# Gathered rows of seven experts turned by DMA instead of TensorE

## The chip, the cores and the metric

The kernel runs on one core of a Trainium2 chip. The metric is the device time of one execution in microseconds; before the change the median of three runs is 1160.86 us (1159.09 to 1165.01).

## What is computed

Three layers follow each other: attention over 4 x 12 heads of 448 x 64, a dense layer with an ELU between its two matrices, and a layer of eight experts. Only the last one matters here:

```python
def _moe2_ref(x, w_gate, w1, w2):          # x (1792, 768), E = 8, F = 1024
    cap = N // E                            # 224 tokens for every expert
    ...                                     # greedy assignment by logits
    for e in range(E):
        mask = assigned == e
        h = np.maximum(x[mask] @ w1[e], 0.0)
        out[mask] = h @ w2[e]
```

## The kernel before

Every float32 factor is split into two float16 numbers, a high and a low one, and a product is made of three float16 products (high by high, low by high, high by low). The rows of x stand in DRAM as `x2_d[0]` and `x2_d[1]`, each with 384 of the 768 columns, high halves first and low halves behind them, so a row of one of them has 768 float16 numbers.

The loop over the experts (lines 974 to 979) does this for each expert `e`:

- `load_expert(e + 1)` brings w1 and w2 in 14 float32 pieces (six of 512 KB, eight of 384 KB) on SP's queue into three staging buffers `st`. ACT (line 350) writes each piece's high half, DVE (line 351) its low half; DVE's instruction frees the staging buffer. There are two sets of weight buffers for odd and even experts, so w1 of expert e + 1 can be written once the first products of expert e - 1 are over, and w2 once its second products are.
- `gather(e + 1)` fetches 224 rows in four parts, `i` (which of the two column halves) by `hh` (which 112 tokens). For each part POOL issues an indirect DMA into one of four buffers `xg` (112 tokens x 768), TensorE turns six blocks of 112 x 128 into the PSUM tile `pte`, and one copy (ACT where hh is 0, DVE where it is 1) brings them to `xT[i]`, named `xTe` in the profile. `xT[i]` has two buffers, so that of expert e + 1 is the one that expert e - 1 has used.
- `expert(e)` makes the first products `phe` (144 matmuls of 224 columns, in four steps of 36; each step needs one of two PSUM tiles, which `relu` on ACT, line 941, and DVE, line 942, reads into `hT`), then the second products `pye` (96 matmuls in two halves), which ACT and DVE copy to `yo` (lines 965 and 966) and POOL scatters to the output (line 967).

Expert 0 is special: its first products run in two halves, because its second column half arrives late.

Nobody writes the order on an engine by hand. A scheduler simulates the program and puts each engine's instructions in a fixed order; an instruction that comes earlier in the program goes first where several are ready. Each engine and each queue then runs its instructions strictly in that order, and waits at the first one that isn't ready. SP's queue carries all weight pieces of this stage. Transposing DMAs on that queue are in use already in the attention stage, at lines 490 (`kT`, `qT`) and 614 (`wt`, 128 rows of 768).

Of the kernel before, what the change touches and what calls it, by code (L numbers as in the profile page):

```python
# [255 lines left out]
def kernel(  # L256
# [14 lines left out]
    nc = tc.nc  # L271
# [19 lines left out]
    HD = CAP // 2  # L291
# [39 lines left out]
    def tr16(o, i, n):  # L331
        mm(o, i, id16[:n, :n], is_transpose=True, start=True, stop=True)
# [404 lines left out]
    for b in range(B):  # L737
        xT = big.tile([P, KC, 2, S], F16, name="xT")
        for hp in range(0, NP, 2):
            d = Duo(b, hp, xT)  # L740
            t = (b * NP + hp) * PR
# [150 lines left out]
    def load_expert(e):  # L892
        if e == 0:
            hold.append(R.marks[0])
        pool = wuB if e % 2 else wuA
        W1 = pool.tile([P, 2, KC, F1], F16, tag="wu", name=f"w1_{e}")
        W2 = pool.tile([P, 2, NF1, DM], F16, tag="wu", name=f"w2_{e}")
        for c in range(KC):
            load_split(W1[:, 0, c, :], W1[:, 1, c, :], w1[e, c * P:(c + 1) * P, :])
        for c in range(NF1):  # L900
            load_split(W2[:, 0, c, :], W2[:, 1, c, :], w2[e, c * P:(c + 1) * P, :])
        return W1, W2

    def gather(e):

        xT = [exg.tile([P, 2, KH, CAP], F16, name=f"xTe{i}") for i in range(2)]
        for i in range(2):
            for hh in range(2):
                xg = exg.tile([HD, 2, DH], F16, name="xg", bufs=4)
                POOL.indirect_dma_start(  # L910
                    out=xg.rearrange("p z d -> p (z d)"), out_offset=None, in_=x2_d[i],
                    in_offset=bass.IndirectOffsetOnAxis(ap=idx[:, 0, 2 * e + hh:2 * e + hh + 1], axis=0))
                pt = psX.tile([P, 2, KH, HD], F16, tag="pt", name="pte")
                for z in range(2):
                    for c in range(KH):
                        tr16(pt[:, z, c, :], xg[:, z, c * P:(c + 1) * P], HD)
                (DVE.tensor_copy if hh else ACT.copy)(xT[i][:, :, :, hh * HD:(hh + 1) * HD], pt)  # L917
        return xT
# [3 lines left out]
    def expert(e, W1, W2, xT):  # L922
# [33 lines left out]
        for hh in range(2):  # L956
# [15 lines left out]
            stores.append(st)  # L972

    W, xT = load_expert(0), gather(0)
    for e in range(NE):
        W_, x_ = W, xT
        if e + 1 < NE:
            W, xT = load_expert(e + 1), gather(e + 1)
        expert(e, *W_, x_)
# [30 lines left out]
```

## Time and profile before

| | us |
|---|---|
| median of three runs | 1160.86 |
| profiled execution, its own time | 1164.11 |
| its span, first to last instruction | 1162.4 |
| PE busy | 1039.3 |
| DVE busy | 784.2 |
| ACT busy | 539.2 |
| POOL busy | 353.9 |
| mean granted clock of TensorE | 0.963 of 2.4 GHz |

In the profile PE is TensorE's matmuls, PEld its weight loads, DVE VectorE, ACT ScalarE, POOL GpSimd and SP SyncE, which here only issues DMAs. A time in brackets behind an instruction is how long its engine stood idle before it, and what ended that. The experts run from about 895 us to the end of the span.

### The profile page before, as it was taken

What the parts mean: (1) busy time and instruction counts of PE and PEld (TensorE: products, weight loads), DVE (VectorE), ACT (ScalarE), POOL (GpSimd) and SP (SyncE); (2) the same over time, 40 slices, a digit from 0 to 9 for tenths busy, and PEclk for the clock granted to TensorE, in tenths of its full rate; (3) what the DMA queues carried; (4) which work ended last, traced back from release to release, by engine and by line L of the source; (5) the groups of instructions that cost most, each with busy time, mean ns of one, the idle gap of its engine ahead of it and who ended that gap; (6) DMA issues with size and microseconds to landing.
All of it is one profiled execution on the core that took longest, in us unless ns stands there. A gap on an engine that the chain in (4) does not pass through costs nothing.

```text
span 1162.4 us, 19353 instructions
## 1 busy us (share of the span) xinstructions
PE 1039.3 (89%) x7030; PEld 608.4 (52%) x7030; DVE 784.2 (67%) x1567; ACT 539.2 (46%) x1099; POOL 353.9 (30%) x462
## 2 busy tenths in 40 slices
PE   0687879897989999999999699999999898999997
PEld 0233334343444445444444345555546687888885
DVE  3788898999988775554337777877775565556520
ACT  2676677776777664554430410011102455555520
POOL 3687775757746451220000000000000412222100
PEclk9888889998999989999999899999999899999999
DMA  6355575569997825336823641030003778778710
GB/s 172 78 133 132 147 207 151 145 178 255 245 256 195 194 68 121 81 95 225 328 55 113 194 167 50 21 130 21 22 21 101 239 236 263 223 244 258 237 47 24
DMA packets 190319, 176.48 MB, mean 152 GB/s; under 512 B 114704, under 2 KB 161808, under 8 KB 189456
## 3 DMA queue, kind: packets, MB, share of 16 engines
q1 hardware_dynamic: 186064, 163.78, 49.5%
q0 software_dynamic: 3328, 11.01, 3.0%
q8 instruction: 55, 0.90, 0.3%
q10 hardware_dynamic: 832, 0.46, 0.1%
q14 instruction: 40, 0.33, 0.1%
HBM read 125.92 MB, written 31.98 MB: 136 GB/s over the span
## 4 chain that ended last, share of the span: by engine, by line
PE 48%; DVE 16%; DMA 13%; issue 10%; ACT 6%; POOL 4%; SPq 2%; POOLq 0%; DVEq 0%; ACTq 0%
PE py L324 17%; PE ph L324 12%; DMA st<-in_moe_w_dram 7%; PE po L324 4%; PE pye L324 3%; PE phe L324 3%; PE ps L324 3%; PE rt_pc L324 2%; DVE w L351 2%; DVE sm L533 2%; ACT w L350 2%; DVE cv L377 2%; PE pta L324 2%; DMA qn<-in_q_dram 2%; PE pl L324 1%
## 5 line engine op out<-in xcount | busy, mean ns | idle before, releaser
L324 PE MATMUL ph<-xT,w_in 128*128 128x448 f16 x1152 | 246.1, 358 | 8.2 <-DVE elu_g L685 5.2
L324 PE MATMUL py<-w_out,g 128*128 128x384 f16 x1152 | 204.5, 329 | 0.0
L324 PEld LDWEIGHTS <-w_in 128*128 128x128 f16 x1152 | 107.7, 99 | 127.7 <-issue 46.1
L351 DVE SCALAR_TENSOR_TENSOR w<-st,w 128x768 f16<-128x768 f32 (+1 forms) x112 | 119.2, 1072 | 76.7 <-ACT w L350 71.5
L545 POOL TENSOR_SCALAR pe<-pe,sm 128x448 f32<-128x448 f32 x168 | 126.7, 764 | 138.8 <-DVE sm L541 70.3
L324 PEld LDWEIGHTS <-g 128*128 128x128 f16 x1152 | 107.4, 98 | 89.3 <-issue 26.7
L324 PE MATMUL ps<-kT,qT 64*128 64x448 f16 (+1 forms) x576 | 97.0, 392 | 56.2 <-ACT pe L535 30.7
L350 ACT ACTIVATE w<-st 128x768 f16<-128x768 f32 (+1 forms) x112 | 103.6, 933 | 90.8 <-DMA st<-in_moe_w_dram 86.5
L535 ACT ACTIVATE pe<-ps,sm 128x448 f32<-128x448 f32 x168 | 105.9, 634 | 50.0 <-DVE sm L533 47.4
L324 PE MATMUL pye<-w,hT 128*112 128x512 f16 (+1 forms) x768 | 126.4, 326 | 0.0
L324 PEld LDWEIGHTS <-w 128*128 128x128 f16 x1152 | 111.8, 100 | 3.3 <-DVE xTe L917 1.2
L127 DVE TENSOR_SCALAR rt_C<-rt_row,rt_m 128x1792 f16<-128x1792 f32 x98 | 107.2, 1149 | 8.2 <-PE rt_pc L324 7.4
L324 PE MATMUL phe<-xTe,w 128*128 128x224 f16 x1080 | 111.4, 264 | 1.1 <-DVE xTe L917 1.1
L533 DVE TENSOR_REDUCE sm<-ps 128x1 f32<-128x448 f32 x168 | 100.2, 615 | 17.2 <-PE ps L324 15.2
L324 PEld LDWEIGHTS <-hT 128*112 128x112 f16 x768 | 91.6, 130 | 32.2
L815 ACT ACTIVATE xh<-py 128x384 f16<-128x384 f32 x28 | 13.7, 491 | 175.0 <-PE py L324 158.1
L324 PEld LDWEIGHTS <-qT 64*128 64x128 f16 (+1 forms) x576 | 27.7, 102 | 99.9 <-issue 66.7
L324 PE MATMUL pta<-id,pe 128*128 128x128 f32 x384 | 64.4, 289 | 15.1 <-POOL pe L545 5.8
L967 POOL DMA_INDIRECT out_dram<-yo,idx x16 | 19.5, 1220 | 179.6 <-DVE yo L966 178.0
L685 DVE SCALAR_TENSOR_TENSOR elu_g<-ph,elu_e 128x448 f32<-128x448 f32 x64 | 39.6, 619 | 48.3 <-ACT elu_e L683 48.1
L324 PEld LDWEIGHTS pta<-id,pe 128*128 128x128 f32 x384 | 45.2, 146 | 44.3 <-POOL pe L545 14.7
L201 POOL MEMSET rt_c<- 128x8 f16 x8 | 0.9, 123 | 220.7 <-DVE rt_c L207 216.6
(176 smaller groups left out, 1470.0 us busy)
## 6 DMA issues: line engine op xcount, KB each, us to landing
st<-in_moe_w_dram SPq DMA_DIRECT2D x48, 512.0 KB
st<-in_moe_w_dram SPq DMA_DIRECT2D x64, 384.0 KB
st<-in_moe_w_in_dram SPq DMA_DIRECT2D x24, 512.0 KB
g_d<-gt SPq DMA_DIRECT2D x64, 192.0 KB
g<-g_d SPq DMA_DIRECT2D x16, 768.0 KB
st<-in_moe_w_out_dram SPq DMA_DIRECT2D x16, 512.0 KB
gl<-g_d SPq DMA_DIRECT2D x32, 192.0 KB
wo_d<-wo SPq DMA_DIRECT2D x16, 384.0 KB
```

The source lines that it names most:

```text
L127: i = DVE.tensor_scalar(C.rearrange("p c t -> p (c t)"), row, m[:, s:s + 1], None, op0=ALU.is_le)
L201: nc.gpsimd.memset(c[:, 0:1, :], 0.0)
L324: i = PE_mm(o, l, r, **kw)
L350: ACT.activation(hi, st, AF.Copy, scale=SW)
L351: DVE.scalar_tensor_tensor(lo, st, SW, hi, op0=ALU.mult, op1=ALU.subtract)
L377: DVE.scalar_tensor_tensor(cv, st[:, :, 1], -0x40000000, cv, op0=ALU.bitwise_and, op1=ALU.bitwise_or)
L533: i = DVE.tensor_reduce(out=st[:, 0, u:u + 1], in_=ps[u], axis=AX.X, op=ALU.max, negate=True)
L535: ACT.activation(p[:, u, :], ps[u], AF.Exp, bias=st[:, 0, u:u + 1], accum_out=st[:, 1, u:u + 1])
L545: POOL.tensor_scalar(p[:, u, :], p[:, u, :], st[:, 2, u:u + 1], 1.0, op0=ALU.mult, op1=ALU.mult)
L685: DVE.scalar_tensor_tensor(gf, ph, -SG / SH, e, op0=ALU.mult, op1=ALU.min)
L815: ACT.activation(xh[:, 0], py, AF.Copy, scale=-SX2 / (SG * SW))
L967: st = POOL.indirect_dma_start(out=out, out_offset=bass.IndirectOffsetOnAxis(ap=idx[:, 1, 2 * e + hh:2 * e + hh + 1], axis=0), in_=yo, in_ ...
```

## The change

In `gather`, for every expert but the first, the six TensorE transposes of a part and the copy behind them are replaced by one DMA on SP's queue. It reads the 112 x 768 buffer `xg` and writes its transpose, 128 x 6 x 112, straight to the part's place in `xT[i]`. The gather itself stays on POOL.

```diff
                 POOL.indirect_dma_start(
                     out=xg.rearrange("p z d -> p (z d)"), out_offset=None, in_=x2_d[i],
                     in_offset=bass.IndirectOffsetOnAxis(ap=idx[:, 0, 2 * e + hh:2 * e + hh + 1], axis=0))
+                if e:
+                    nc.sync.dma_start_transpose(
+                        xT[i].rearrange("p z c t -> p (z c) t")[:, :, hh * HD:(hh + 1) * HD],
+                        xg.rearrange("p z d -> p (z d)"))
+                    continue
+
                 pt = psX.tile([P, 2, KH, HD], F16, tag="pt", name="pte")
```

## Rows read from the trace of the kernel before

**Rows 1.** The page's head and its part 1, whole span.
```profile
span 1162.4 us, 19353 instructions
PE 1039.3 (89%) x7030; PEld 608.4 (52%) x7030; DVE 784.2 (67%) x1567; ACT 539.2 (46%) x1099; POOL 353.9 (30%) x462
```

**Rows 2.** Stretches: length, busy us (instructions) of each engine, clock, DMA share, GB/s.
```profile
1032.00:1063.00 31.00, 30.13 (x263) 26.00 (x262) 17.99 (x23) 17.03 (x22) 6.82 (x7) 1.00 0.81 253
1063.00:1094.00 31.00, 31.00 (x269) 26.71 (x267) 19.46 (x23) 17.03 (x22) 7.46 (x6) 1.00 0.83 256
1094.00:1125.00 31.00, 31.00 (x269) 26.70 (x267) 11.41 (x16) 10.80 (x16) 2.38 (x2) 1.00 0.33 109
```

**Rows 3.** Chain of waits, 975 to 1033 us: start, length, what ran.
```profile
975.43 10.86 PE phe L324 x96
...
1001.90 0.59 PE pte L324 x12
...
1007.59 9.30 PE phe L324 x97
1016.89 15.60 PE pye L324 x96
1032.49 0.61 PE pte L324 x12
```

**Rows 4.** Instructions on tile pte: count, shortest/median/longest ns, first and last start.
```profile
L324 PE MATMUL pte<-id,xg x192: 209/213/301, 893.4 to 1100.2; 112*128 112x112 f16 x192
L917 ACT COPY xTe<-pte x16: 700/712/723, 894.0 to 1098.9; 128x672 f16<-128x672 f16 x16
L917 DVE COPY xTe<-pte x16: 499/503/509, 894.7 to 1100.7; 128x672 f16<-128x672 f16 x16
```

**Rows 5.** Tile wt, the timeline at 403 us, DMA from 404.5 to 406.5.
```profile
L614 SPq DMA_TRANSPOSE wt<-wo x32: 1212/1242/2232, 249.4 to 403.5; - x32
403.54 1.22 SPq L614 DMA_TRANSPOSE wt<-wo  x1
DMA  0000459999999999999999752000000000000000
DMA packets 800, 0.20 MB, mean 98 GB/s; under 512 B 800, under 2 KB 800, under 8 KB 800
```

**Rows 6.** Timeline around PE's gap at 972 us: start, length, what, idle before.
```profile
969.73 2.27 PE L324 MATMUL phe<-xTe,w 128*128 128x224 f16 x22
973.48 0.84 ACT L350 ACTIVATE w<-st 128x768 f16<-128x768 f32 x1 [2.76 <-DMA st<-in_moe_w_dram]
974.23 1.32 ACT L917 COPY xTe<-pte 128x672 f16<-128x672 f16 x2
974.98 0.45 PE L324 MATMUL pte<-id,xg 112*128 112x112 f16 x6 [2.98 <-ACT xTe L917]
975.44 0.56 ACT L941 ACTIVATE hT<-phe 128x448 f16<-128x448 f32 x1
```

**Rows 7.** ACT's and DVE's timeline in the first products of expert 3.
```profile
1010.80 0.84 ACT L350 ACTIVATE w<-st 128x768 f16<-128x768 f32 x1 [1.25 <-DMA st<-in_moe_w_dram]
1011.55 0.53 ACT L941 ACTIVATE hT<-phe 128x448 f16<-128x448 f32 x1
1012.55 0.62 DVE L942 SCALAR_TENSOR_TENSOR hT<-phe,hT 128x448 f16<-128x448 f32 x1
```

**Rows 8.** ACT's timeline: its wait ahead of yo's second half, two of four.
```profile
1001.93 0.60 ACT L965 ACTIVATE yo<-pye 112x512 f32<-112x512 f32 x1 [4.65 <-PE pye L324]
1064.15 0.60 ACT L965 ACTIVATE yo<-pye 112x512 f32<-112x512 f32 x1 [1.63 <-PE pye L324]
```

**Rows 9.** Waits of SP's queue, 886 us to the end: total, times, longest.
```profile
SPq L362 <- DVE w L351: 132.5, 79, 5.3
```

**Rows 10.** Timeline of POOL: first and last of expert 1's four gathers.
```profile
904.61 0.93 POOL L910 DMA_INDIRECT xg<-x_d,idx  x1 [0.30 <-issue]
909.79 0.93 POOL L910 DMA_INDIRECT xg<-x_d,idx  x1 [0.75 <-PE pte L324]
```

## Prediction

> **What bounds the kernel now.** I read the page's shares first, then the stage that the diff touches. Over the whole span PE is busy for 89%, more than any other engine [rows 1]; but a share of the span says nothing of one stage, so the next view is the table of stretches over the experts. There PE is busy for 30.1 to 31.0 of each 31 us at the full clock, 2.4 GHz, while DVE has 18 to 19 us, ACT 17 and POOL 7 [rows 2]. The chain of waits, followed through one expert, shows the same: products of the gathered rows (pte), first products (phe), second products (pye), and the next expert's pte, almost without a break [rows 3]. So between 938 us and the end TensorE sets the pace, and what is taken off it there can come off the time.
>
> Two more things have to be seen in these views, because they decide how much of it does. The 16 DMA engines are busy for 0.81 and 0.83 of two of these stretches, and for 0.33 once the weights of the last expert are in [rows 2]: the weight stream is the second limit, and close. And in the order of ACT the relu of an expert stands behind splits of weight pieces; a split waits for its piece to land, the relu waits behind it, and PE needs the relu to get a PSUM tile free [rows 6, 7]. Through that order a late weight piece stops PE, although the weights themselves are wanted only an expert later.
>
> **What the change takes away.** Of 192 products pte, 24 belong to expert 0 and stay; 168 go [rows 4]. The profile gives 213 ns for one, but they are pipelined; on the chain twelve of them take 0.59 us, so 49 ns each [rows 3]. 168 x 0.049 = 8.3 us of PE time, in seven portions of 1.2 us. All of it lies where PE is dense, so it lies on the path. ACT loses 14 copies of 0.712 us, DVE 14 of 0.503 us [rows 4], 10.0 and 7.0 us; neither engine is the limit, so by themselves these count nothing, but two of ACT's stand ahead of a relu, which counts below.
>
> **PE's gap at 972 us.** PE finished 22 products at 972.0 and waited 2.98 us for a copy of ACT, which stood behind a split that had waited 2.76 us for its weight piece [rows 6]. Without pte PE would go on: 24 more products of this step's 72 (48 are done) at 9.30 / 97 = 0.096 us, 2.3 us, to 974.3. Then it needs the relu that ACT now begins at 975.44; without the two copies (1.32 us) ahead of it that is 974.1, with 0.56 us of its own and 0.62 us for DVE's half it is done at about 975.3. PE would wait 1.0 us in place of 2.98: 1.9 us gained. Behind the gap 96 products took 10.86 us, where 97 take 9.30 us later on [rows 3]; I don't count these 1.6 us, since a shorter stop is left. Bounds for the gap as a whole: nothing, if the piece lands later still, and 4.6 us.
>
> **What the change adds.** There are 28 transposing DMAs, four for an expert. The nearest row is wt, which has 128 rows of 768 where the new ones have 112: SP needs 1.24 us to issue one, 2.23 us at worst [rows 5]. One that ran with nothing else kept the DMA engines busy for about 19 of 40 slices of 0.05 us, 0.95 us for 0.20 MB [rows 5]; 112 rows make 0.83 us of that. An expert thus costs SP 4 x 1.24 = 5.0 us (8.9 at worst) and the DMA engines 4 x 0.83 = 3.3 us. No row shows a transpose of 112 rows; I take the scaled value, and keep the unscaled one, 3.8, and none below 3.3, as nothing is smaller than the packets that must move.
>
> In a stretch of 31 us the DMA engines now work 0.82 x 31 = 25.4 us. With 3.3 us more and 1.2 us less time that is 28.7 of 29.8, 0.96. This fits, but barely; it is why the forecast isn't the whole 8.3 us.
>
> What is the cover? A transpose for expert e + 1 can start once expert e - 1 has made its first products, for then xT's buffer is free; its rows were gathered before that. It is wanted when the second products of e - 1 and both kinds of expert e are over: 15.6 + 13.8 + 15.6 = 45 us later, from the chain [rows 3] (13.8 is 144 products at 0.096). So PE never waits for a transpose itself, unless it stands far behind in SP's queue. Behind it on that queue stand the next weight pieces. SP waits for DVE to free a staging buffer for 132.5 us, 79 times [rows 9], so it has idle time; and at the moment that xT comes free three pieces are staged already and SP and the DMA engines have little to do. There the four transposes fit: 5.0 us, while ACT and DVE split the three pieces that are there. The gathers of the next expert then wait for the transposes, which free xg, not for PE; they move out of the first products into the second ones.
>
> How much delay can the weight stream bear? ACT waits at the end of the second products for PE: between 4.65 and 1.63 us in four experts, of which the largest and the smallest are shown [rows 8]. That is the slack of the stream in one expert, about 3.1 us as the middle of the two. A delay inside it costs nothing.
>
> **Where the gain can be eaten.** In expert 3 the relu that frees the tile for the fourth step is over at 1013.17 [rows 7]. PE comes to that step after 108 products and 24 pte, at 1002.49 + 108 x 0.096 + 0.6 = 1013.4 [rows 3]: 0.3 us to spare. Taking 1.2 us from PE alone would make it wait 0.9 us of them. Whether it does depends on the fifth piece, for which ACT waited 1.25 us just ahead of the relu [rows 7]: it lands earlier if the gathers are gone from there and later if the transposes fall there. Between 0 and 0.9 us for each of five experts while weights stream, 0 to 4.5 us; I take the middle, 2.2.
>
> **Expert 1.** Its gathers are issued from 904.61 to 909.79 us [rows 10], while its weights still stream, so its four transposes stand among those pieces, and there is no slack of a whole expert yet. Between nothing and 5.0 us; I take 1.0, for the nearest row is the wait of ACT for a piece in such a place, 1.25 [rows 7].
>
> **The sum.** 8.3 + 1.9 - 2.2 - 1.0 = 7.0 us, so the profiled execution's 1164.1 us (span 1162.4, 1.7 around it) would become 1157.1. That execution lies 3.2 us above the median of the three runs; against the median of 1160.9 I forecast 1153.9, say 1154.
>
> **A rule that speaks against this.** A transpose by DMA shows in this trace as 0.95 us of DMA time for six blocks of 128 x 128 [rows 5]. The Trainium skill, in "VectorE: DVE Perf Modes", section The three transpose paths, gives 390 ns for one 128 x 128 block on TensorE and 1309 ns by DMA, and advises TensorE where PSUM will do. By that figure 24 blocks would be an estimate of 31 us of DMA an expert, which would not fit beside the weights; the trace, with six blocks in 0.95 us, doesn't agree with it as a cost of each block in a large transpose.
>
> **The rivals.**
>
> *The weight stream eats the gain.* The transposes delay the pieces by about the slack, relus stay where they are, and PE waits for them in place of pte. Then nothing is gained while weights stream; what is left are the portions at the two ends, that of expert 1 and that of expert 7, whose rows are turned when the stream is nearly over: 2 x 1.2 = 2.4 us, 1158.5. For it: DMA at 0.96 and relus with 0.3 us to spare. Against it: ACT and DVE lose the copies there, and the gathers move away. Chance 0.31.
>
> *SP's queue holds up the weights: slower.* Place: a transpose at the head of SP's queue, with weight pieces behind it, each followed by a split and a relu in ACT's order. Price: 5.0 us of SP in one piece, of which 3.1 are covered by the slack, so 1.9 us for each of five experts, 9.5, less the 2.4 us of the ends: 7 us more than now, 1168. It decides from the point where the transposes cost the stream over 3.1 + 1.2 = 4.3 us an expert: then it loses more than PE gains. It comes if the scheduler puts them between the pieces of w2, during first products, or ahead of gathers that land late. Chance 0.22.
>
> *The whole gain.* The stream copes, the gap goes with its slow clock: 8.3 + 4.6 = 12.9 us, 1148. This is the upper end of my forecast, with its chance.
>
> *A transpose of 112 rows doesn't run like one of 128,* but block by block. If a block costs what a whole transpose of the trace takes on the DMA engines, 0.95 us [rows 5], 24 make 23 us an expert; with 25.4 us of other DMA that is 48 us, 18 more than the period, and six experts make over 100 us: 1270. Nothing in the trace speaks for it; 112 is a multiple of 16 as 128 is. The rule of the Trainium skill above would act in this way. Chance 0.01.
>
> **How the numbers follow.** Forecast 0.46, gain eaten 0.31, slower by SP's queue 0.22, block by block 0.01. About 0.5%, 5.8 us, is what a measurement of this kernel can tell from no change. The forecast lies beyond it, so faster 0.46, same 0.31, slower 0.23. The likeliest case alone reaches from 1148 to 1155; the range for 8 in 10 takes in the other two: from 1146 (the whole gain, with the 1 to 2 us by which runs differ) to 1168.
>
> **What would show it.** Right: no pte after 920 us; 28 transposes on SP of some 1.2 us, most just after the end of first products; PE's cycle of an expert at 29.4 us in place of 30.6; gathers during second products; DMA share near 0.95. Wrong: idle time of PE ahead of phe, ended by ACT's or DVE's hT, with ACT waiting for st just ahead of it; long SP entries of a transpose that waits for xg with weight pieces behind it; w2's last split no longer ahead of the end of second products. If PE waits for the DMA of xT itself, my account of the cover is wrong.

## The result and the profile after

The changed kernel takes 1170.36 us, the median of five runs (1164.72 to 1173.98), where the kernel before takes 1162.52 us beside it (1159.09 to 1165.01): a ratio of 1.0074, 95% interval 1.0046 to 1.0101 (intervals in brackets below are of the same kind). It is slower by some 8 us. The profiled execution of after is the one of 1164.72 us, 5.6 under its median, and its span is only 0.6 us longer than before's [rows 1]. That hides where the loss is: its experts began earlier (first second product at 918.25 us against 922.57), and from the last second product of expert 0 to that of expert 7 it took 221.4 us against 216.5. So 4.9 us are lost inside the experts that the profile can show. Where the rest of the 8 us arises no profile shows, as the profiled execution is the fastest of the five.

The page's head and the busy time of PE, then three stretches, columns as in [rows 2]:

```profile
span 1163.0 us, 19039 instructions
PE 1032.5 (89%) x6862; PEld 600.8 (52%) x6862; DVE 778.1 (67%) x1553; ACT 530.4 (46%) x1085; POOL 356.0 (31%) x462
```

```profile
970.00:1001.00 31.00, 26.31 (x179) 21.03 (x179) 16.72 (x20) 14.94 (x19) 7.05 (x6) 0.89 0.91 259
1032.00:1063.00 31.00, 28.10 (x226) 23.60 (x224) 17.58 (x20) 14.95 (x20) 6.86 (x6) 1.00 0.90 267
1063.00:1094.00 31.00, 28.28 (x222) 24.02 (x221) 17.74 (x20) 16.15 (x21) 1.82 (x3) 0.94 0.83 247
```

The 168 products are gone (6862 of 7030), and PE is busy for 6.8 us less over the span. But in the stretches where it had 30.1 and 31.0 us of 31 [rows 2], it now has 28.1 and 28.3, and two of the three stretches have a lower granted clock (0.89 and 0.94). The work that was taken off PE has become idle time of PE. The waits from 886 us to the end (engine, line, what it waited for: total, times, longest) say of what; first one line of before, then three of after:

```profile
ACT w L350 <- DMA st<-in_moe_w_dram: 74.0, 67, 4.6
```

```profile
ACT w L350 <- DMA st<-in_moe_w_dram: 96.5, 74, 4.9
POOL xg L910 <- DMA xTe<-xg: 95.0, 11, 20.3
PE phe L324 <- DVE hT L948: 11.8, 6, 5.2
```

PE never waits for a tile that a DMA has turned. It waits 11.8 us for a relu (hT), and ACT waits for weight pieces longer than it did (96.5 us against 74.0). How one leads to the other is in the timelines of PE and ACT, here as expert 5 begins:

```profile
1062.54 7.06 PE L324 MATMUL phe<-xTe,w 128*128 128x224 f16 x72
1072.33 5.27 PE L324 MATMUL phe<-xTe,w 128*128 128x224 f16 x36 [2.72 <-DVE hT L948]
```

```profile
1062.47 1.06 ACT L350 ACTIVATE w<-st 128x1024 f16<-128x1024 f32 x1 [1.51 <-DMA st<-in_moe_w_dram]
...
1068.12 0.84 ACT L350 ACTIVATE w<-st 128x768 f16<-128x768 f32 x1 [2.39 <-DMA st<-in_moe_w_dram]
1069.90 0.84 ACT L350 ACTIVATE w<-st 128x768 f16<-128x768 f32 x1 [0.94 <-DMA st<-in_moe_w_dram]
1070.65 0.53 ACT L947 ACTIVATE hT<-phe 128x448 f16<-128x448 f32 x1
```

PE first, then ACT. The last piece of w1 (1024 columns) is split at 1062.47, when the second products end; so the first pieces of w2 (768) are late too, ACT waits 2.39 and 0.94 us for them, and the relu that PE needs stands behind them, at 1070.65. PE stops for 2.72 us.

What made the pieces late is on SP's queue (start, length, what) and in the chain of waits that follows from there:

```profile
970.07 14.47 SPq L362 DMA_DIRECT2D st<-in_moe_w_dram  x8
984.63 5.57 SPq L914 DMA_TRANSPOSE xTe<-xg  x4
990.29 8.00 SPq L362 DMA_DIRECT2D st<-in_moe_w_dram  x5
```

```profile
981.31 3.46 PE phe L324 x36
984.78 1.07 SPq L914
...
988.93 1.27 SPq L914
990.29 3.84 DMA st<-in_moe_w_dram
994.15 1.07 ACT w L350
...
997.96 5.31 DMA st<-in_moe_w_dram
1003.30 0.85 ACT w L350
1004.17 0.97 DVE w L351
1005.16 3.49 DMA st<-in_moe_w_dram
1008.67 0.85 ACT w L350
1009.54 0.97 DVE w L351
1010.53 5.08 DMA st<-in_moe_w_dram
```

The four transposes stand where I had put them, right at the end of first products (984.78). But from there the chain does not go back to PE. It goes through SP's transposes to a weight piece, its split on ACT and DVE, and then round the three staging buffers: 997.96, 1005.16, 1010.53, two rounds in 12.6 us, 6.3 each. A buffer that comes free after 6.3 us, and three of them, make 2.1 us a piece and 29.4 us for 14, by estimate: as long as PE's 29.4 us for an expert. All nine rounds of this view, 990.29 to 1048.53 us, have a mean of 6.5 us, which makes about 30. Grouped by line, the chain between 960 and 1050 us shows how the bound changed; before, after, and two experiments that come below (e8, no transpose at all; e10, six staging buffers):

```profile
by line: PE pye L324 34.7%; PE phe L324 27.4%; DMA st<-in_moe_w_dram 26.9%; DVE w L351 5.9%; ACT w L350 5.2%; PE pte L324 2.5%; issue 1.4%; ACT xTe L917 0.7%; DVE yo L966 0.5%; SPq L362 0.4%; DVE xTe L917 0.0%; DVEq L351 0.0%
```

```profile
by line: DMA st<-in_moe_w_dram 50.0%; DVE w L351 13.0%; PE phe L324 11.0%; ACT w L350 10.2%; SPq L914 7.2%; issue 7.0%; SPq L362 0.7%; DVE yo L972 0.7%; DVE hT L948 0.6%; PE pye L324 0.2%; DVEq L351 0.1%
```

```profile
by line: DMA st<-in_moe_w_dram 54.3%; PE pye L324 16.3%; DVE w L351 13.6%; ACT w L350 12.2%; PE phe L324 4.0%; issue 1.3%; DVE hT L951 0.7%; ACT yo L974 0.7%
```

```profile
by line: PE pye L324 47.1%; PE phe L324 45.1%; issue 4.5%; DMA xTe<-xg 3.8%; POOL xg L918 0.7%; POOLq L918 0.0%
```

Before, PE has 65% of it (34.7 + 27.4 + 2.5), pieces and their splits 38%: 14.8 us ahead of PE's gap [rows 6] and 19.4 us from 1034 us on. A chain is followed back from what ended last in the window, here a landing at 1054 us, so the second part says that the stream ran close beside PE, and not that PE waited for it. After, PE has 11% and pieces, splits and SP's transposes 80% (50.0 + 13.0 + 10.2 + 7.2). In e8, with nothing turned at all, pieces and splits still have 80%; in e10 PE has 92%. The shares of this view can sum to a little over 100.

The measure used from here on is the period of an expert: the time between the last second products of successive experts, from the 768 rows of tile pye (96 for each expert), in us. "Middle" is the mean of experts 3 to 5, "sum" that of all seven. Each row is one profiled execution; the times further down are medians of several.

| kernel | 1 | 2 | 3 | 4 | 5 | 6 | 7 | middle | sum |
|---|---|---|---|---|---|---|---|---|---|
| before | 28.3 | 35.3 | 30.6 | 31.6 | 30.7 | 30.6 | 29.4 | 31.0 | 216.5 |
| after | 28.6 | 37.6 | 29.9 | 32.6 | 33.9 | 29.4 | 29.4 | 32.2 | 221.4 |
| e1, no turn | 32.2 | 36.3 | 29.4 | 29.6 | 30.0 | 29.9 | 29.4 | 29.7 | 216.8 |
| e8, no turn, gathers paced | 27.7 | 32.3 | 30.4 | 30.2 | 30.3 | 29.6 | 29.4 | 30.3 | 209.9 |
| e2, plain DMAs | 30.2 | 33.6 | 34.7 | 31.3 | 30.8 | 30.6 | 29.4 | 32.3 | 220.6 |
| e13, a sixth of each transpose | 29.6 | 36.8 | 31.1 | 32.2 | 31.7 | 32.0 | 29.4 | 31.7 | 222.7 |
| e3, transposes spread | 28.5 | 35.2 | 30.3 | 34.5 | 30.5 | 30.4 | 29.4 | 31.7 | 218.6 |
| e9, before, six buffers | 30.1 | 30.5 | 30.7 | 30.5 | 30.7 | 30.0 | 29.4 | 30.6 | 211.8 |
| e10, after, six buffers | 32.0 | 29.4 | 29.4 | 29.4 | 29.4 | 29.4 | 29.4 | 29.4 | 208.4 |
| e15, before, six from expert 3 | 30.4 | 30.7 | 30.6 | 30.6 | 30.6 | 30.3 | 29.4 | 30.6 | 212.7 |
| e14, after, six from expert 3 | 34.7 | 30.5 | 29.4 | 29.4 | 29.4 | 29.4 | 29.4 | 29.4 | 212.2 |

### The profile page after: what moved, and what is told of

Read it like the earlier page. It is cut to its first block, busy times and chain, and to the rows that moved or that the text cites. A ratio compares the mean times of both kernels' runs of the same rounds, so it can differ in the third digit from the quotient of the medians.

```text
span 1163.0 us, 19039 instructions
## 1 busy us (share of the span) xinstructions
PE 1032.5 (89%) x6862; PEld 600.8 (52%) x6862; DVE 778.1 (67%) x1553; ACT 530.4 (46%) x1085; POOL 356.0 (31%) x462
## 4 chain that ended last, share of the span: by engine, by line
PE 42%; DVE 17%; DMA 14%; issue 13%; ACT 6%; POOL 4%; SPq 3%; POOLq 0%; DVEq 0%; ACTq 0%
PE py L324 17%; PE ph L324 10%; DMA st<-in_moe_w_dram 8%; PE po L324 3%; PE ps L324 2%; PE rt_pc L324 2%; DVE sm L533 2%; DVE w L351 2%; ACT w L350 2%; PE pta L324 2%; DMA wt<-wo 2%; DVE cv L377 2%; DMA qn<-in_q_dram 2%; PE pl L324 1%; PE phe L324 1%
## 5 line engine op out<-in xcount | busy, mean ns | idle before, releaser
L324 PE MATMUL ps<-kT,qT 64*128 64x448 f16 (+1 forms) x576 | 94.4, 385 | 53.5 <-ACT pe L535 28.1
L324 PE MATMUL phe<-xTe,w 128*128 128x224 f16 x1080 | 113.5, 268 | 13.4 <-DVE hT L948 11.8
L324 PEld LDWEIGHTS <-w 128*128 128x128 f16 x1152 | 114.3, 101 | 18.9 <-issue 13.0
L324 PEld LDWEIGHTS <-hT 128*112 128x112 f16 x768 | 91.7, 130 | 31.7
L910 POOL DMA_INDIRECT xg<-x_d,idx x32 | 38.2, 1193 | 167.1 <-DMA xTe<-xg 95.0
```

The lines of the kernel that those rows point to most:

```text
L324: i = PE_mm(o, l, r, **kw)
L910: POOL.indirect_dma_start(out=xg.rearrange("p z d -> p (z d)"), out_offset=None, in_=x2_d[i], in_offset=bass.IndirectOffsetOnAxis(ap=idx[: ...
```

## The experiments

The theory: three staging buffers make the weight stream as slow as PE, so the block of transposes ahead of the fourth piece delays splits and relus (the rival that forecast slower). The others: it is the traffic of the transposes; it is the order of relus behind splits; it is the gathers that the change lets run earlier. The expectations call them by short names: "queue" (SP is held ahead of the pieces), "staging" (three buffers are too few), "engine" (traffic), "order" (relus). A ratio is against the kernel before on the same chip.

**No turning at all.** In e1 experts 1 to 7 read the rows of expert 0; nothing is turned for them, by either engine. In e8 the gathers, which then wait for nothing, are also bound to the scatters of three experts earlier.

```diff
-        xT = [exg.tile([P, 2, KH, CAP], F16, name=f"xTe{i}") for i in range(2)]
+        xT = first                              (expert 0's two tiles, for every expert)
         ...
+                if e > 2:                       (e8 only)
+                    tc.add_manual_dep(d.ins, stores[2 * (e - 3) + i].ins.name, NOSYNC, reason="pace")
+                if e:
+                    continue
```

> Experts 1 to 7 read expert 0's turned rows; their own rows are still gathered, but neither TensorE nor a DMA turns them, so the outputs of experts 1 to 7 are those of other rows. It gives the most that taking the 168 products away can bring. Queue theory (the four transposes hold SP's queue, and that delays the weight pieces) and engine theory (their packets load the DMA engines): without transposes nothing is delayed, and the time falls by the 8.3 us of the products up to 13 us, to 1150 to 1154 where before has 1162.5. Order theory (relus stand behind splits, so PE can't run faster than the weight stream whatever is done to it): the fall is 2 to 5 us, and PE waits 0.9 us or more for hT in most experts.

> Nothing is turned for experts 1 to 7, as in the first experiment, so their outputs are those of other rows; but POOL's gathers go in the order that the kernel before has, tied to its scatters, where the first experiment let those of all experts run in the first 80 us. If its gain of nothing came from that crowd of gathers (PE waited 6.5 us there), it now shows: 1152 to 1157. If PE can't run faster than the weight stream whatever is taken off it (order theory): 1161 to 1165.

e1: 1164.58 us, ratio 1.0002 (0.9981 to 1.0023). e8: 1161.07, ratio 0.9973 (0.9955 to 0.9991). With all 8.3 us of products gone and no transpose in their place, nothing is gained in e1 and 3 us in e8. That is far from the 1150 to 1154 that the queue theory alone had for e1: more than SP's hold keeps PE back. In e8 PE waits six times from expert 1 on, 4.2 us in all, each time for a relu; the two largest stand in expert 2:

```profile
975.04 3.61 PE L324 MATMUL phe<-xTe,w 128*128 128x224 f16 x36 [1.88 <-DVE hT L951]
980.33 3.61 PE L324 MATMUL phe<-xTe,w 128*128 128x224 f16 x36 [0.71 <-DVE hT L951]
```

Its middle period is 30.3 us, 0.3 us less than the 30.6 that PE needed before, where PE alone would need 29.4. In e1 all gathers are issued by 953 us, so none runs beside the middle experts, and there the same three buffers keep up with 29.7 us; a stretch of it, columns as in [rows 2]:

```profile
1001.00:1032.00 31.00, 31.00 (x252) 26.45 (x251) 17.67 (x21) 15.57 (x20) 1.71 (x2) 1.00 0.71 227
```

So the stream had next to no slack: 0.3 us an expert beside the gathers that the kernel needs, about 0.9 without them. That e1 is worse than e8 in experts 1 and 2 (68.5 us against 60.0) goes with its gathers, which run in one crowd up to 953 us; pacing them is all that e8 changes.

**A plain DMA, and a small transpose.** e2 moves 112 x 672 untransposed in place of each transpose (the rows are then not turned, a part left out). e13 keeps instruction, place and waits, but turns one block of six from expert 2 on; the rest keeps older rows. Both hold the turned rows in two fixed pairs of tiles.

```diff
-                    nc.sync.dma_start_transpose(                                      (e2)
+                    nc.sync.dma_start(xT[i].rearrange("p z c t -> p (z c) t")[0:HD, :, hh * HD:(hh + 1) * HD],
+                        xg.rearrange("p z d -> p (z d)")[:, 0:2 * KH * HD].rearrange("p (c t) -> p c t", t=HD))
```

```diff
+                    n = 2 * KH if e == 1 else 1                                       (e13)
                     nc.sync.dma_start_transpose(
-                        ...[:, :, hh * HD:(hh + 1) * HD], xg.rearrange("p z d -> p (z d)"))
+                        ...[:, 0:n, hh * HD:(hh + 1) * HD], xg.rearrange("p z d -> p (z d)")[:, 0:n * P])
```

> Each transposing DMA is replaced by a plain DMA of the same buffer to the same place: 112 x 672 numbers in runs of 224 bytes, so nearly the same bytes and packets, but not transposed; 96 of 768 columns of a part are left out, and the products of experts 1 to 7 use wrong numbers. Queue theory: a plain DMA holds SP for some 0.35 to 0.5 us, not 1.25, so four hold it for 2 us or less, within the slack; the time falls to 1152 to 1157. Engine theory: the DMA engines have the same packets to move, so the time stays near the changed kernel's, 1168 to 1172.

> As the changed kernel, but from expert 2 on each of the four transposes of an expert turns only its first block of six (128 of the 768 columns); the other blocks keep expert 0's or 1's rows, so part of the computation is left out. Place, waits and number of the instructions stay, the DMA engines have a sixth of their work. If the loss comes from the traffic of the transposes beside the weight pieces, the period of the middle experts falls from 32.1 us (mean of 29.9, 32.6, 33.9) to the 30.3 us of the kernel that turns nothing, and the time to about 1162. If it comes from SP, which is held per instruction ahead of the fourth piece, an entry of SP stays near 1.2 us, the period stays at 31.5 to 32.5, and the time at 1168 to 1171. If SP's hold grows with the blocks, an entry is shorter and the period lies between.

e2: 1171.75 us, ratio 1.0060 (1.0038 to 1.0082). e13: 1172.15, ratio 1.0068 (1.0040 to 1.0096). Both are as slow as the change. Tile xTe (shortest, median, longest ns) in after and in e13, and a block of four on SP's queue in e2 and e13:

```profile
L914 SPq DMA_TRANSPOSE xTe<-xg x28: 1202/1259/1814, 907.2 to 1085.1; - x28
```

```profile
L919 SPq DMA_TRANSPOSE xTe<-xg x28: 1097/1192/1829, 911.4 to 1089.9; - x28
```

```profile
1021.93 4.81 SPq L921 DMA_DIRECT2D xTe<-xg  x4
```

```profile
1022.25 4.93 SPq L919 DMA_TRANSPOSE xTe<-xg  x4
```

A sixth of the traffic takes the DMA share back to 0.76 to 0.80 of the stretches from 970 to 1094 us, and changes little else: SP is held 4.9 to 5.7 us instead of 5.3 to 6.0, the middle period is 31.7 us and the sum no smaller than after's. So neither the traffic nor the turning costs the time. It is four DMAs in a row on SP's queue ahead of the fourth piece. I expected the plain DMAs to hold SP for less, and one alone does:

```profile
L921 SPq DMA_DIRECT2D xTe<-xg x28: 601/637/2632, 910.5 to 1086.7; - x28
```

But in a block of four the last was held for up to 2.63 us, so that four took 4.4 to 4.9 us. Why it is held stays open.

**Another place on the queue.** e3 binds each transpose behind one weight piece, from the fourth to the seventh of its expert; e12 leaves every first half on TensorE.

```diff
+                    tc.add_manual_dep(d.ins, pieces[14 * e + 3 + 2 * i + hh].ins.name, NOSYNC, reason="behind a piece")
```

```diff
-                if e:
+                if e and hh:                                                          (e12)
```

> The changed kernel with one more order: the four transposes of an expert don't go in one block ahead of its fourth weight piece, but one each behind the fourth, fifth, sixth and seventh piece. All is computed. Queue theory: SP is held for 1.25 us at a time, in gaps in which it would wait for DVE to free a buffer (1 to 2 us), the fourth piece is issued 3 us earlier than in the changed kernel; the time falls below before's, to 1153 to 1159. Engine theory: the packets are the same, 1167 to 1172. Order theory: 1158 to 1162.

> Three staging buffers; for experts 1 to 7 only the parts with hh = 1, whose copy DVE made, are turned by DMA, the others by TensorE and ACT as before. All is computed. It takes half of the products away (4.2 us) and adds half of the transposes (2.5 us of SP and 1.7 us of DMA for an expert). If the stream of pieces is the bound, each transpose lengthens it: between before and the changed kernel, 1165 to 1168. If the stream has slack that two transposes fit into: 1158 to 1162.

e3: 1164.95 us, ratio 1.0001 (0.9977 to 1.0025). e12: 1169.68, ratio 1.0043 (1.0020 to 1.0067). Spreading gives back what the block costs, and no more: the fourth piece is issued 2.8 to 5.3 us after the end of first products, as before (2.8 to 5.6), where after the change it was 5.2 to 8.6 (from the issue rows of experts 4 to 7). But pieces behind it are later, and PE still waits:

```profile
976.66 5.27 PE L324 MATMUL phe<-xTe,w 128*128 128x224 f16 x36 [3.94 <-DVE hT L953]
1041.39 5.27 PE L324 MATMUL phe<-xTe,w 128*128 128x224 f16 x36 [3.26 <-DVE hT L953]
```

In e12 half the transposes cost about half; PE also waits once, 3.21 us, for a copy of ACT ahead of its own products.

**The order of relus.** e4 gives the first products three PSUM tiles instead of two (pte keeps one). e5, e6 and e7 order the splits of w2 behind the relus: in the kernel before, in the changed one, and in a spread one.

```diff
-        ACT.activation(hi, st, AF.Copy, scale=SW)
+        a = ACT.activation(hi, st, AF.Copy, scale=SW)
+        for x, y in zip((a, d), relus[-1:] and relus[-1]):
+            tc.add_manual_dep(x.ins, y.ins.name, NOSYNC, reason="behind a relu")
     ...                                         (e5 to e7: w2's pieces are loaded from relu to relu)
```

```diff
-    ... psX.tile([P, 2, CAP], F32, tag="ph", name="phe") ...                          (e4)
+    ... psX.tile([P, 2, CAP], F32, tag="ph", name="phe", bufs=3) ...
```

> The changed kernel with three PSUM tiles for first products in place of two, and one in place of two for expert 0's transposes: PE needs the first relu a step of 3.4 us later. All is computed; the block of four transposes stays. If PE's waits for hT (2 to 5 us in four experts) are what costs the time, as queue and engine theory both say, they fall to between 0 and 2 us each and the time to 1155 to 1161. If something else costs it (weights that are late themselves, the wait for a gather), it stays at 1167 to 1172.

> The kernel before, with its TensorE transposes, but the order on ACT and DVE is bound: of the eight pieces of w2 that are split during an expert's first products, two may go ahead of the first relu, two more behind it, then two, one and one behind the next three. A relu so stands behind at most two splits that wait for a piece. All is computed. Order theory (relus behind splits tie PE to the weight stream): PE's waits, 3 to 5 us with the slow clock behind them, go; 1155 to 1160 where before has 1162 to 1164. If the stream itself is the bound, without regard to the order, nothing changes, or it gets worse by 2 to 5 us, as splits now wait for relus.

> The changed kernel with the same bound order of relus and splits; the transposes go in blocks of three and one. All is computed. Order theory: the stream still loses 3 us an expert to the transposes, but PE is tied to it by two pieces only and uses the lead of a whole expert that the weights have; 1152 to 1160, below before's 1162 to 1164. If the stream is the bound in itself, or the lead is used up, it stays near the changed kernel's 1168 to 1172.

> The bound order, and the transposes spread: one behind the fourth, one behind the fifth and two behind the sixth weight piece. All is computed. Order theory and queue theory together: the 8.3 us of the products come off nearly whole, 1150 to 1156. If the stream is the bound: 1162 to 1166, as the spread kernel without the bound order had 1165.

e4: 1171.78 us, ratio 1.0051 (1.0031 to 1.0071). e5: 1165.76, 1.0010 (0.9993 to 1.0027). e6: 1182.04, 1.0143 (1.0119 to 1.0168). e7: 1171.25, 1.0055 (1.0029 to 1.0081). None gains. In e4 the waits move: PE comes further before it stops, part of it then at its second products,

```profile
989.39 0.86 PE L324 MATMUL pye<-w,hT 128*112 128x512 f16 x4 [1.24 <-ACT hT L947]
```

and in e6 ACT waits 106.9 us for pieces (96.5 after): splits held behind relus free the staging buffers later. e6 and e7 are slower than either theory had forecast. So the relu's place only says where a late stream stops PE, not whether. As the cause of the loss this theory falls.

**Deeper staging.** From expert 2 on (e9, e10, e11), or expert 3 (e14, e15), pieces alternate between two pools of three buffers. e9 and e15 are the kernel before with this, e10 and e14 the changed one, e11 the changed one with spread transposes.

```diff
-            st = stg.tile([P, w], F32, tag="st", name="st")
+            pool = stg
+            if wide:
+                pool = wide[wide[0] % 2 + 1]
+                wide[0] += 1
+            st = pool.tile([P, w], F32, tag="st", name="st")
     ...
+    stgx = ctx.enter_context(tc.tile_pool(name="stgx", bufs=3))
     ...
+        if e == 2:                              (e14, e15: 3)
+            wide.extend((0, stg, stgx))
```

> The kernel before with six staging buffers for the weight pieces of experts 2 to 7 in place of three. All is computed. Staging theory: a piece goes round from its issue over landing (3.2 to 4.8 us), ACT's split (0.85 to 1.06), DVE's (0.96 to 1.23) and some waiting, about 6.5 us; with three buffers that is a piece each 2.2 us, 30.3 us for 14, and this round, not PE, sets the period of 30.6 us. With six buffers PE's own work sets it (30.6 us with the 1.2 us of pte), the long waits at about 972 us and the slow clock behind them go: 1154 to 1160 where before has 1162 to 1164. If the DMA engines are the bound (engine theory): no change.

> The changed kernel with six staging buffers. All is computed. Staging theory: the transposes' time hides behind pieces that are staged already, PE's period falls to 29.4 us, and the change shows its 8.3 us against the kernel before with six buffers: 1147 to 1153. Engine theory (the transposes' packets, 3.3 us an expert, fill the DMA engines): 1160 to 1170, slower than the kernel before with six buffers.

> Six staging buffers, and the transposes spread: one behind each of the first four pieces of w2. All is computed. Staging theory: 1146 to 1152, at most 2 us below the block of four. Engine theory: as the block of four.

> Six staging buffers with the change, but used from expert 3 on in place of expert 2, so that no piece is staged earlier while expert 0 waits for its gathered rows. If earlier pieces of expert 2 are what made expert 0 wait 7.5 us for its rows, that wait falls back to 4 to 5 us, and the time from 1157.1 to about 1154 to 1156; the periods of the last five experts stay at 29.4 us. If expert 2's pieces are as much in need of the deep staging as the rest (its transposes stand ahead of its pieces while expert 0 runs), the period of expert 2 grows to 34 to 38 us again and the time to 1160 or more.

> The kernel before with six staging buffers from expert 3 on. With them PE alone should set its periods of the last experts: 30.6 us, 29.4 of products and 1.2 of pte, 1.2 us more for each than with the change. If expert 0's wait falls back to 5 us, the time is 1159 to 1162; against the same edit with the change it should be 5 to 8 us slower.

e10: 1157.08 us (1153.20 to 1162.86), ratio 0.9949 (0.9924 to 0.9973), faster than both kernels. e9: 1163.70, 0.9996 (0.9972 to 1.0020). e11: 1165.53, 1.0030 (1.0003 to 1.0057). e14: 1161.78, 0.9967 (0.9943 to 0.9992). e15: 1165.95, 0.9998 (0.9972 to 1.0025). With six buffers the same change is worth 6.6 us (e10 against e9) and 4.2 us (e14 against e15), less than the 8.3 of the products. About what is missing stands in expert 1, which takes 2.0 us longer in e10 than in e9 and 4.4 longer in e14 than in e15. e10 also settles two rivals: the traffic and the gathers, bound to the transposes as in after, are there, and the time falls. One stretch of e9 and one period of e10:

```profile
1000.50:1031.00 30.50, 30.50 (x267) 26.47 (x266) 18.54 (x23) 16.24 (x22) 8.29 (x7) 1.00 0.78 258
```

```profile
999.70:1029.10 29.40, 29.40 (x243) 25.25 (x241) 17.17 (x20) 14.90 (x22) 7.72 (x6) 1.00 0.95 289
```

PE is busy without a gap in both. The transposes stand in e10 where they stood in after (a block of 5.19 us at 1013.42, first products end at 1014.25), and cost nothing in these periods, because the fourth to sixth pieces of w1 were issued 3.5 to 7.6 us before them (issue rows of experts 4 to 7). The first w2 piece follows 4.4 to 5.3 us after the end of first products, where it came 11.4 to 14.8 us after it in after; ACT has six of them to split without a wait when the second products of expert 3 end, and the relu behind them comes soon:

```profile
1029.09 4.50 ACT L351 ACTIVATE w<-st 128x768 f16<-128x768 f32 x6
1033.49 0.53 ACT L955 ACTIVATE hT<-phe 128x448 f16<-128x448 f32 x1
```

In e11, with transposes bound behind the seventh to tenth piece, the eleventh and twelfth are issued 1.0 to 1.5 us later than in e10 (experts 4 to 7), and PE waits again, I take it for those pieces. Its 1165.5 us are far from the 1146 to 1152 that I expected:

```profile
1012.59 5.27 PE L324 MATMUL phe<-xTe,w 128*128 128x224 f16 x36 [2.33 <-DVE hT L960]
1076.09 3.61 PE L324 MATMUL phe<-xTe,w 128*128 128x224 f16 x36 [2.87 <-DVE hT L960]
```

So place and depth belong together: of the two places tried with six buffers, the block at the head, with pieces standing ahead of it, was the better.

e9's experts gain (211.8 us over seven periods, before 216.5) but its time doesn't; by its time alone it would speak for the engine theory, which e10 rules out. Expert 0 waits longer there for its own gathered rows, 6.50 and 1.70 us against 4.8 and 0.9; I took earlier staged pieces of expert 2 for the cause. e14 and e15 were made for that, and it falls; their waits are as long:

```profile
911.91 0.74 PE L324 MATMUL pte<-id,xg 112*128 112x112 f16 x6 [7.27 <-DMA xg<-x_d,idx]
```

```profile
912.68 0.74 PE L324 MATMUL pte<-id,xg 112*128 112x112 f16 x6 [6.30 <-DMA xg<-x_d,idx]
```

What makes this wait differ between kernels that are alike up to there stays open. It is about 2 us of each comparison with the kernel before; e10 against e9 and e14 against e15 have it on both sides.

## Why the prediction was wrong, point by point

**What is taken away: right.** 49 ns a product and 1.2 us an expert. With the stream out of the way the period falls from 30.6 to 29.4 us, as forecast, and in e10 for six experts in a row.

**What is added: nearly right for SP, short for the DMA engines.** 1.24 us of SP for each, 5.0 an expert, was forecast; 1.26 and, for a block of four, 5.3 to 6.0 came. For the DMA engines 3.3 us an expert was forecast, from wt alone on an idle queue [rows 5]. From the two stretches above, 0.95 x 29.4 - 0.78 x 30.5 = 4.1 us, an estimate. The share of 0.95 in e10 is what I forecast (0.96), and it fits.

The Trainium skill, "VectorE: DVE Perf Modes", The three transpose paths, gives 1309 ns for a 128 x 128 block by DMA; by that figure 24 blocks an expert would be an estimate of 31 us. The trace doesn't agree: 24 blocks cost 4.1 us of the DMA engines in e10.

**Cover: right as far as it went.** PE waits for no tile that a DMA has turned in after, and in experts 4 to 7 the block begins between 0.8 us ahead of the end of first products and 3.2 us behind it.

**The slack of the weight stream: wrong, and this is the step that failed.** I read 3.1 us of slack from ACT's waits ahead of yo's second half [rows 8]. That wait shows that ACT is early at one point of the order, once its pieces have come; it does not show that the stream could come later. It shows in e8, where PE with 1.2 us less to do came only 30.6 - 30.3 = 0.3 us an expert forward, and in e1, where it came 0.9 forward with no gathers beside it: 0.3 to 0.9 us in place of 3.1. Because of the 3.1 us the sum puts a delay of the stream at nothing; its 2.2 us stand only for relus that a faster PE comes to too early. The profile had a sign of it in a view that I cut too short. My chain ran over 975 to 1033 us, where PE is nearly all of it [rows 3]; from 960 to 1050 pieces and splits have 38% of it. And the DMA share of 0.81 [rows 2] doesn't count what bounds the staging buffers, used in a ring, which is a buffer's round: a landing of 3.5 to 5.3 us, 0.85 for ACT, 0.97 for DVE, and then the next issue. With three pieces in flight at most, the DMA engines had a share of only 0.82 and 0.83 in e8 (990 to 1050.6 us), where PE still waited for a relu, 0.70 us at 1010.74; with six it was 0.91 to 0.95 in e10.

**"SP and the DMA engines have little to do" there: wrong.** Before the change SP issued its next piece 2.8 to 5.6 us after that moment. With four transposes ahead of it, it was issued after 5.2 to 8.6 us, 2.4 us later by the means of experts 4 to 7 (6.7 against 4.3), and the ring, which has hardly any slack, passes that on to splits, relus and PE.

**The gap at 972 us: wrong in sign.** 1.9 us were to be gained. The wait of 2.98 us for a copy of ACT behind a late split [rows 6] became one of 5.20 us, now for a relu behind late splits, and the 36 products behind it took 6.41 us instead of 3.61:

```profile
974.69 6.41 PE L324 MATMUL phe<-xTe,w 128*128 128x224 f16 x36 [5.20 <-DVE hT L948]
```

The working moved ACT's copies out of the way, and left the piece as early as it was.

**Where the gain can be eaten: right place, far too small.** 2.2 us for five experts. PE's waits for relus sum to 11.8 us. The account of the profile nearly closes with them: from the end of expert 0 PE's work falls by 6 x 1.2 = 7.1 us and the time grows by 4.9, so 12.0 us are new. Waits are 7.9 us more (11.8, less 2.98 and 0.9 before), slow products 2.9 more (2.8 and 1.7 behind the two longest waits, less the 1.6 behind [rows 6]'s): 10.8 of the 12.0. The remaining 1.2 us I can't place.

**Expert 1: can't be told apart.** Its period grew by 0.3 us, but the waits of expert 2 are 2.2 us longer; 1.0 was forecast. With six buffers for the later pieces expert 1 takes 2.0 us longer with the change (e10 against e9) and 4.4 (e14 against e15).

**The rival that was right** is the one that SP's queue holds up the weights: 7 us and 1168 were forecast for it, 8 us and 1170 came. Its place and mechanism held, its condition (transposes that cost the stream more than 4.3 us an expert) did not: the piece came 2.4 us later, against a slack of 0.3 to 0.9. From which delay on it decides, no run measures. The middle periods grew by 32.2 - 31.0 = 1.2 us against before, where the rival had 1.9. That its total comes so near is in part luck: its delay was too large by 2.6 us and its slack by 2.2 to 2.8, and the two errors offset each other. I gave it 0.22 because I set 5.0 us against a slack that I had not measured.

## What to carry to other kernels

Before work is moved onto a queue that also feeds a ring of buffers, work out the round of the ring (landing, consumers, next issue, divided by the number of buffers) and set it against the period of the bounding engine: a wait of a consumer somewhere in its order is no slack, and a DMA share below one isn't either. Follow the chain of waits over more than one period and group it by line, for a second limit close behind the first shows there. If the ring has no slack, deepen it together with the change: here the same diff cost 8 us with three staging buffers, and brought 6.6 us with six against the same depth without it (4.2 where the six came in an expert later).

## What the runs showed of the hardware

- A transposing DMA held SP's queue by the instruction far more than by its size: 1.19 us for one block (e13), 1.26 for six (after; both medians). A plain DMA of 112 x 672 numbers held it for 0.64 us (median in e2), but for up to 2.63 as the last of four, and a weight piece of 128 rows for 0.33 us (1017.49 us in after).
- TensorE's clock: in after, behind a wait of 2.17 us (1039.15 us) 36 products took 3.61 us, in a stretch with a granted clock of 1.00, the level of 2.4 GHz. Behind 2.72 us they took 5.27 and behind 5.20 us 6.41, in stretches with means of 0.94 and 0.89, between the two levels of 2.4 and 1.2 GHz. A stop of PE so cost up to 2.8 us beyond itself. Its length alone doesn't decide this: in e11 36 products took 5.27 us behind 2.33 us, and 3.61 behind 2.87.
- Traffic of the transposes beside the weights is nearly free here: cut to a sixth (e13), the DMA share fell from between 0.83 and 0.91 to between 0.76 and 0.80 in the stretches from 970 to 1094 us, the middle period from 32.2 to 31.7 us only, and the time not at all. Gathers beside the weights are not quite free: the middle period was 30.3 us with them (e8) and 29.7 without (e1).
